# Layer 2's second products as seven products of halves, its narrow block first

## The chip, the cores and the metric

One NeuronCore of a Trainium2 chip runs the whole program. It has five engines that work beside each other and wait for each other by semaphores: TensorE (PE in the profile) multiplies and writes to PSUM, VectorE (DVE) and ScalarE (ACT) work element by element, SyncE (SP) issues the DMA transfers, and GpSimd (POOL) has nothing to do here. The metric is the device time of one execution in microseconds, the median of three runs.

## The reference

Attention with two kinds of masks (four heads see the last 32 positions, four see every 32nd), then two MLPs on the 2304 tokens that it gives, each with a squared relu:

```
attn = softmax(mask(q @ k.T / 8)) @ v            # 4 batches, 8 heads, 576 positions, 64 wide
x    = attn as (2304, 512)
x    = relu(x @ moe_w_in)**2  @ moe_w_out         # 512 -> 2048 -> 512
out  = relu(x @ moe2_w_in)**2 @ moe2_w_out        # 512 -> 2048 -> 512
```

## The kernel before

Numbers are split in two: a high part, rounded to the format fp32r in which TensorE multiplies here, and a low part, the remainder. A product of two numbers is three products on TensorE, high by high, low by high and high by low. So each value that TensorE reads is made in two operations: ScalarE copies it to fp32r (the high part), VectorE subtracts that from the value (the low part).

An MLP layer runs over blocks of 512 tokens and one narrow block of 256 (BLOCKS), and in a block over 16 pieces f of 128 of the 2048 hidden columns; a narrow block takes two pieces in one step. One step is

- the first product, mm1: 12 products of 512 columns (24 of 256 in a narrow block) into a PSUM bank ps_h. Then ScalarE takes the relu (r), ScalarE and VectorE each square it (gh, the high part, and sq), and VectorE makes the low part gl = sq - gh;
- the second product, mm2: 12 products of 512 columns that add up over the 16 steps in four PSUM banks ps_y. In layer 2 the squared values are the stationary operand and w_out streams; in layer 1 the other way round. At a block's end ScalarE copies the banks out (o) and a DMA stores them.

The main loop issues mm1(s + 1) before mm2(s), so that one step's products cover the making of the next step's values. Every engine takes its instructions in the order in which the code issues them (there is no scheduler), so that order is written by hand: attention of later batches, loading and conversion of weights and the splitting of layer 2's input (load_y, split_y, which read layer 1's result back from y_dram) are put in at numbered places (point) between groups of products.

Weights arrive as 64-bit words; a piece of 128 x 512 is converted in four operations in a row (sign_and_end: two on VectorE; exponent_range: ScalarE; together: VectorE; in_parts: a copy on ScalarE and a subtraction on VectorE), each piece one place behind the next. Layer 2's 32 pieces are loaded during layer 1's last block and converted there and in layer 2's first block. Attention takes the first three blocks along.

SBUF is nearly full, so buffers are shared under tags: x tiles (three pairs), the attention's buffers (qk0, qk1, qk2), the squared values (gh, gl, two each).

## Time and profile before

| | before |
|---|---|
| median of three runs | 909.28 us (909.27 to 909.30) |
| profiled execution | 909.87 us |
| its span, first to last instruction | 908.1 us |
| TensorE busy | 888.9 us, 98% |
| VectorE busy | 461.6 us, 51% |
| ScalarE busy | 410.3 us, 45% |
| mean granted TensorE clock | 0.994 of full |

The busy time of TensorE counts a product from its start to its modelled end, and products overlap; what one costs in a stream is read from the distance of two starts. Times on the clock of the trace are microseconds from the span's start. Layer 2 begins at about 508 us; its wide blocks run to about 856 us, its narrow block is the last.

### The profile page before, as it was taken

How to read it: one execution, taken by the hardware profiler on the slowest of the kernel's cores; microseconds unless marked ns; L12 is line 12 of the kernel's file. 1: busy time of each engine (PE TensorE's matmuls, PEld its weight loads, DVE VectorE, ACT ScalarE, POOL GpSimd, SP SyncE). 2: the span in 40 equal slices, each digit the busy share in tenths (PEclk: the TensorE clock that was granted, in tenths of full speed). 3: DMA queues.
4: the chain of work that ended last, by engine and by line, in shares of the span. 5: the costliest groups of instructions: out<-in, count | busy, mean ns of one | idle time of the engine just before them, and what ended most of it. 6: DMA issues, size and time to landing. Idle time of an engine off the chain costs nothing.

```text
span 908.1 us, 12461 instructions
## 1 busy us (share of the span) xinstructions
PE 888.9 (98%) x4640; PEld 750.1 (83%) x4640; DVE 461.6 (51%) x1201; ACT 410.3 (45%) x859; POOL 0.2 (0%) x4
## 2 busy tenths in 40 slices
PE   8699999999999999999999999999999999999998
PEld 8578878888888888899888888888888888888897
DVE  5999973477666665222378786322232222223221
ACT  6787863555555544322466766232233222322222
POOL 0000000000000000000000000000000000000000
PEclk9799999999999999999999999999999999999999
DMA  8956510222222120101666500010001000100010
GB/s 268 323 196 215 193 41 19 85 75 93 71 69 102 53 64 11 42 6 37 205 211 203 198 29 24 0 70 1 24 0 70 1 24 1 58 6 6 7 41 24
DMA packets 43885, 71.92 MB, mean 79 GB/s; under 512 B 3504, under 2 KB 28208, under 8 KB 43824
## 3 DMA queue, kind: packets, MB, share of 16 engines
q1 hardware_dynamic: 43824, 71.12, 23.5%
q8 instruction: 37, 0.61, 0.3%
q14 instruction: 24, 0.20, 0.1%
HBM read 61.67 MB, written 9.44 MB: 78 GB/s over the span
## 4 chain that ended last, share of the span: by engine, by line
PE 87%; DVE 9%; ACT 1%; DMA 1%; issue 1%; SPq 0%; ACTq 0%; DVEq 0%
PE ps_h L679 41%; PE ps_y L736 40%; PE ps_o L480 2%; DVE raw L219 2%; DVE w L244 1%; DVE val L230 1%; PE ps_pt L464 1%; PE ps_s L327 1%; DVE raw L216 1%; PE ps_s L421 1%; DVE s L441 1%; DMA qk<-st_qk_d 1%; DVE gl L703 1%; PE ps_x L526 1%; DVE xl L568 0%
## 5 line engine op out<-in xcount | busy, mean ns | idle before, releaser
L679 PE MATMUL ps_h<-xh,w 128*128 128x512 f32 (+1 forms) x1280 | 402.4, 374 | 0.0
L679 PEld LDWEIGHTS ps_h<-xh,w 128*128 128x128 f32 x1280 | 234.2, 189 | 38.5
L693 ACT ACTIVATE r<-ps_h 128x512 f32<-128x512 f32 x144 | 86.1, 598 | 373.1 <-PE ps_h L679 340.8
L702 DVE TENSOR_TENSOR sq<-r 128x512 f32<-128x512 f32 x110 | 76.1, 692 | 336.7 <-ACT r L693 336.6
L679 PE MATMUL ps_h<-xl,w 128*128 128x512 f32 (+1 forms) x640 | 236.5, 370 | 0.0
L736 PE MATMUL ps_y<-gh,w 128*128 128x512 f32 (+1 forms) x640 | 157.5, 376 | 0.0
L736 PE MATMUL ps_y<-w,gh 128*128 128x512 f32 x576 | 144.6, 389 | 0.0
L679 PEld LDWEIGHTS ps_h<-xl,w 128*128 128x128 f32 x640 | 121.3, 190 | 17.3
L736 PEld LDWEIGHTS ps_y<-w,gh 128*128 128x128 f32 x576 | 107.6, 188 | 22.0
L703 DVE TENSOR_TENSOR gl<-sq,gh 128x512 fp32r<-128x512 f32 x144 | 99.7, 692 | 49.8 <-ACT gh L699 36.0
L736 PEld LDWEIGHTS ps_y<-gh,w 128*128 128x128 f32 x640 | 108.2, 188 | 16.5
L736 PE MATMUL ps_y<-gl,w 128*128 128x512 f32 (+1 forms) x320 | 85.4, 374 | 0.0
L736 PE MATMUL ps_y<-w,gl 128*128 128x512 f32 x288 | 79.1, 389 | 0.0
L701 ACT ACTIVATE gh<-r 128x512 fp32r<-128x512 f32 x110 | 69.7, 634 | 3.5
L736 PEld LDWEIGHTS ps_y<-w,gl 128*128 128x128 f32 x288 | 54.1, 188 | 11.3
L736 PEld LDWEIGHTS ps_y<-gl,w 128*128 128x128 f32 x320 | 54.5, 188 | 8.5
L457 ACT ACTIVATE s<-s,m 96x128 f32<-96x128 f32 (+2 forms) x176 | 55.7, 387 | 4.4 <-DVE m L441 3.8
L225 ACT ACTIVATE raw<-raw 128x512 f32<-128x512 f32 x64 | 43.2, 675 | 13.3 <-DVE raw L219 13.3
L480 PEld LDWEIGHTS ps_o<-v,pt 128*96 128x96 f32 (+2 forms) x352 | 42.8, 174 | 7.1 <-ACT pt L472 2.4
L219 DVE SCALAR_TENSOR_TENSOR raw<-raw 128x512 int32<-128x512 int32 x64 | 44.4, 694 | 2.2
L244 DVE TENSOR_TENSOR w<-val,w 128x512 fp32r<-128x512 f32 x64 | 43.7, 683 | 2.6 <-ACT w L243 2.5
L230 DVE SCALAR_TENSOR_TENSOR val<-raw 128x512 int32<-128x512 int32 x64 | 43.7, 684 | 0.0
(39 smaller groups left out, 576.0 us busy)
## 6 DMA issues: line engine op xcount, KB each, us to landing
raw<-moe_w_in_d SPq DMA_DIRECT2D x32, 512.0 KB, 4.9
raw<-moe_w_out_d SPq DMA_DIRECT2D x32, 512.0 KB, 3.9
qk<-loc_qk_d SPq DMA_DIRECT2D x12, 416.0 KB, 3.1
out_d<-o SPq DMA_DIRECT2D x18, 256.0 KB, 2.0
y_dram<-o SPq DMA_DIRECT2D x16, 256.0 KB, 2.0
y_in<-y_dram SPq DMA_DIRECT2D x16, 256.0 KB, 3.0
qk<-loc_qk_d SPq DMA_DIRECT2D x12, 304.0 KB, 4.0
v<-loc_v_d SPq DMA_DIRECT2D x24, 130.0 KB, 2.4
```

The source lines that it names most:

```text
L219: nc.vector.scalar_tensor_tensor(out=lower, in0=upper, scalar=-(2 ** 31), in1=lower, op0=ALU.bitwise_and, op1=ALU.bitwise_or)
L225: nc.scalar.activation(out=upper, in_=upper, func=AF.Copy, scale=2.0 ** (W_EXP // 8 - 112))
L230: nc.vector.scalar_tensor_tensor(out=val[n].bitcast(I32), in0=upper, scalar=3, in1=lower, op0=ALU.logical_shift_left, op1=ALU.bitwise_or,)
L244: nc.vector.tensor_tensor(out=w[:, 1], in0=v, in1=r32(w[:, 0]), op=ALU.subtract)
L457: nc.scalar.activation(out=blk, in_=blk, func=AF.Exp, scale=-1.0, bias=m[:nq, j:j + 1])
L480: nc.tensor.matmul(ps[:nq, j * W:(j + 1) * W], lhsT=pt[:nk, j * nq:(j + 1) * nq], rhs=t[:nk, j * W:(j + 1) * W], start=True, stop=True,)
L679: nc.tensor.matmul(ps[:, e * n:(e + 1) * n], lhsT=w[:, a, c * P:(c + 1) * P], rhs=x[:, c, :n], start=c == 0 and e == 0 and i == 0, stop=c ...
L693: nc.scalar.activation(out=r, in_=ps, func=AF.Relu, scale=W_BACK)
L701: nc.scalar.activation(out=h, in_=r, func=AF.Square)
L702: nc.vector.tensor_tensor(out=sq, in0=r, in1=r, op=ALU.mult)
L703: nc.vector.tensor_tensor(out=lo, in0=sq, in1=r32(h), op=ALU.subtract)
L736: nc.tensor.matmul(y, lhsT=lhsT, rhs=rhs, start=f == 0 and c not in seen, stop=end and m == last[c])
```

## The change

Layer 2's narrow block comes first, and its second product stays as it was, by another way to its operands. In the four wide blocks of layer 2 two steps (an even and an odd f, 256 hidden columns, a pair) are taken together: the 512 x 256 squared values are cut in two by tokens (even and odd) and in two by hidden columns, w_out's 256 x 512 in two by two, and Strassen's scheme makes the product of seven products of halves instead of eight. Each of the seven has its own accumulator bank over the block: four ps_y banks and the three ps_a banks, so that one bank, ps_h, is left for the first products. For each pair VectorE and ScalarE make the sums and differences of the squared values and split them in high and low parts: g_first for the first three products, g_second for the other four. The sums of w_out's pieces are made once, when they are converted (halves), and kept as float32; their high and low parts are made anew for each pair (w_operands; w_direct in the narrow block) into the x tile that layer 2 leaves free. At a block's end seven operations on VectorE (sums) put the output together from the seven banks. The conversion of weights uses all eight places of a step in layer 1's last block instead of six.

```diff
-    [(0, TB), (TB, TB), (2 * TB, TB), (3 * TB, TB), (NT - TB // 2, TB // 2)],
+    [(0, TB // 2)] + [(n * TB + TB // 2, TB) for n in range(4)],
...
+QK_COLS = {"qk0": 1024, "qk1": 1024, "qk2": 768}
+HALF = DM // 2
...
+    def halves(n):
+        kind, layer, f = pieces[n]
+        w = wt[pieces[n]] = wpool.tile([P, 4, HALF], F32, tag=f"w{n % half1}", name="wf")
+        v = val.pop(n).rearrange("p (h m) -> p h m", h=2)
+        sub = nc.vector.tensor_tensor
+        if f % 2 == 0:
+            nc.scalar.activation(out=w[:, 0:4:3], in_=v, func=AF.Copy)
+            sub(out=w[:, 1], in0=v[:, 1], in1=v[:, 0], op=ALU.subtract)
+        else:
+            w0 = wt["out", 1, f - 1]
+            nc.scalar.activation(out=w[:, 0:2], in_=v, func=AF.Copy)
+            sub(out=w0[:, 2], in0=v[:, 1], in1=w0[:, 3], op=ALU.subtract)
+            sub(out=w[:, 2], in0=v[:, 1], in1=w0[:, 1], op=ALU.subtract)
+            sub(out=w[:, 3], in0=w[:, 2], in1=v[:, 0], op=ALU.subtract)
...
+    def x_tile(part, n):
+        return xpool.tile([P, KC, TB], F32R, tag=f"{part}{n}", name=part)
     def x_tiles(j):
         if j not in xh:
-            xh[j] = x_tile("xh", "xh")
-            xl[j] = x_tile("xl", "xl")
+            xh[j], xl[j] = (x_tile(t, j % 3) for t in ("xh", "xl"))
...
-        if s != 1 and n_att[0] < len(att):
+        if s == first_7 + 1 or s != 1 and s < first_7 and n_att[0] == len(att):
+            ps = ps_a.tile([P, TB], F32, tag="a", name="ps_h")
...
+        if s >= first_7:
+            t = sqs[s] = gpool.tile([P, TB], F32, tag=("r", "sq")[s % 2], name="sq", bufs=1)
+            nc.scalar.activation(out=t, in_=ps, func=AF.Relu, scale=W_BACK)
+            nc.vector.tensor_tensor(out=t, in0=t, in1=t, op=ALU.mult)
+            return
...
+    sqs, ga, gb, w_parts, rings, banks = {}, {}, {}, {}, {}, {}
+    first_7 = steps.index((NB + 1, 0))
+    PA, PB = ("11", "s1t1", "s3t3"), ("12", "s4b22", "s2t2", "a22t4")
+    def ring(n):
+        if n not in rings:
+            rings[n] = [x_tile(t, n).rearrange("p c n -> p (c n)") for t in ("xh", "xl")]
+        return rings[n]
+    def w_direct(s):
+        f = steps[s][1]
+        w_parts[s] = []
+        for e in range(2):
+            at = (s % 2 * 2 + e) * 512
+            hi, lo = (x[:, at:at + 512] for x in ring(2))
+            w = ready(("out", 1, f + e))
+            src = w[:, 0:2] if e else w[:, 0:4:3]
+            h3, l3 = (x.rearrange("p (h m) -> p h m", h=2) for x in (hi, lo))
+            parts(h3, l3, src)
+            w_parts[s].append((hi, lo))
...
+    def w_operands(s, first):
+        k, f = steps[s]
+        n = 1 if k == len(blocks) - 1 and f % 4 == 1 else 2
+        wr = w_parts[s] = [x[:, 48:48 + 7 * HALF] for x in ring(n)]
+        w = ready(("out", 1, f - 1)), ready(("out", 1, f))
+        src, a, e = (w[0][:, 0:3], 0, 3) if first else (w[1], 3, 7)
+        hi, lo = (x[:, a * HALF:e * HALF] for x in wr)
+        parts(hi, lo, src.rearrange("p i m -> p (i m)"))
+    def quarters(s):
+        return [t.rearrange("p (n e) -> p e n", e=2) for t in (sqs[s - 1], sqs[s])]
+    def parts(hi, lo, src):
+        nc.scalar.activation(out=hi, in_=src, func=AF.Copy)
+        nc.vector.tensor_tensor(out=lo, in0=src, in1=r32(hi), op=ALU.subtract)
+    def g_first(s):
+        a1, a2 = quarters(s)
+        n = TB // 2
+        h = fpool.tile([P, 3 * HALF], F32R, tag="qk2", name="gah", bufs=1)
+        lo = gpool.tile([P, 3 * HALF], F32R, tag="gl", name="gal", bufs=2)
+        h, lo = ga[s] = [x.rearrange("p (i n) -> p i n", i=3) for x in (h, lo)]
+        s13, s42 = (
+            gpool.tile([P, TB + P], F32, tag="gh", name="s", bufs=2)[:, :2 * n].rearrange(
+                "p (i n) -> p i n", i=2)
+            for _ in range(2)
+        )
+        parts(h[:, 0], lo[:, 0], a1[:, 0])
+        tt = nc.vector.tensor_tensor
+        tt(out=s13[:, 0], in0=a1[:, 1], in1=a2[:, 1], op=ALU.add)
+        tt(out=s13[:, 1], in0=a1[:, 0], in1=a1[:, 1], op=ALU.subtract)
+        nc.scalar.activation(out=h[:, 1:3], in_=s13, func=AF.Copy)
+        tt(out=s42[:, 1], in0=s13[:, 0], in1=a1[:, 0], op=ALU.subtract)
+        tt(out=lo[:, 1:3], in0=s13, in1=r32(h[:, 1:3]), op=ALU.subtract)
+        tt(out=s42[:, 0], in0=a2[:, 0], in1=s42[:, 1], op=ALU.subtract)
+        gb[s] = s42
+    def g_second(s):
+        _, a2 = quarters(s)
+        s42 = gb[s]
+        h = fpool.tile([P, 4 * HALF], F32R, tag="qk0", name="gbh", bufs=1)
+        lo = fpool.tile([P, 4 * HALF], F32R, tag="qk1", name="gbl", bufs=1)
+        h, lo = gb[s] = [x.rearrange("p (i n) -> p i n", i=4) for x in (h, lo)]
+        parts(h[:, 0:4:3], lo[:, 0:4:3], a2)
+        parts(h[:, 1:3], lo[:, 1:3], s42)
+        if steps[s][0] < len(blocks) - 1 or steps[s][1] == 1:
+            w_operands(s, False)
...
+    def products(s, which, point):
+        k, f = steps[s]
+        nt = TB // 2 // P
+        first, end = f == 1, f == NF - 1
+        wr = w_parts[s]
...
+        if first:
+            tags = ("y0", "y1", "y2") if which == 0 else ("y3", "a", "a", "a")
+            for name, tag in zip(names, tags):
+                pool = ps_a if tag == "a" else ps_y
+                banks[name] = pool.tile([P, 512], F32, tag=tag, name="ps_y")
+        at = range(len(names)) if which == 0 else (2, 0, 3, 1)
+        for i in at:
+            y = banks[names[i]]
+            cols = slice((w0 + i) * HALF, (w0 + i + 1) * HALF)
+            for t in range(nt):
+                rows = slice(t * P, (t + 1) * P)
+                for m, (a, w) in enumerate(((h, wr[0]), (h, wr[1]), (lo, wr[0]))):
+                    nc.tensor.matmul(
+                        y[:, t * HALF:(t + 1) * HALF],
+                        lhsT=a[:, i, rows],
+                        rhs=w[:, cols],
+                        start=first and t == 0 and m == 0,
+                        stop=end and t == nt - 1 and m == 2,
+                    )
+            point()
+            if end:
+                sums(k, names[i])
...
+        if name == "11":
+            acc["p1"] = tile_of("pt")
+            nc.scalar.activation(out=acc["p1"], in_=banks[name], func=AF.Copy, scale=W_BACK)
+        elif name == "s2t2":
+            u2, u3, c22 = acc["u2"], acc["u3"], acc["c22"] = tile_of("pt"), tile_of("s"), tile_of("s")
+            add(u2, name, acc["p1"])
+            add(u3, "s3t3", u2)
+            add(c22, "s1t1", u3)
+            store(c22, 1, 1)
+            add(u2, "s1t1", u2)
+        elif name == "12":
+            add(acc["p1"], name, acc["p1"])
+            store(acc["p1"], 0, 0)
+        elif name == "a22t4":
+            add(acc["u3"], name, acc["u3"], -1.0)
+            store(acc["u3"], 1, 0)
+        elif name == "s4b22":
+            add(acc["u2"], name, acc["u2"])
+            store(acc["u2"], 0, 1)
...
+    def layer_2(s, point):
+        k, f = steps[s]
+        if s < first_7:
+            if s + 1 < first_7:
+                w_direct(s + 1)
+            mm2(s, point)
+        elif f % 2 == 0:
+            g_first(s + 1)
+            if s == first_7:
+                w_operands(s + 1, True)
+            else:
+                products(s - 1, 1, point)
+            g_second(s + 1)
+        else:
+            products(s, 0, point)
+            if s + 1 == len(steps):
+                products(s, 1, point)
+                return
+            w_operands(s + 2, True)
+            if steps[s + 2][0] == len(blocks) - 1 and steps[s + 2][1] > 1:
+                w_operands(s + 2, False)
...
-        s -= 12
+        s, lag, each = (first[NB], 2, 1) if k == NB + 1 else (s - 12, 3, 2)
...
-                elif (layer == 1 or j == NB - 1 and f > 2) and n_pt[0] % 4:
+                elif j == NB - 1 and f > 2 and layer == 0 or layer == 1 and n_pt[0] % 4:
...
-            mm1(s + 1, point)
+            if s == first[NB] - 1:
+                w_direct(s + 1)
+            if s != first_7:
+                mm1(s + 1, point)
+            if s == first_7 - 1:
+                mm1(s + 2, point)
             point()
-            mm2(s, point)
+            if layer == 0:
+                mm2(s, point)
+            else:
+                layer_2(s, point)
```

How the instructions stand, at three places.

VectorE in a steady part of a wide block of layer 2, before: two steps, with sq the square and gl its low part, and between them the low part of a piece of the next block's input.

```order
L702 TENSOR_TENSOR sq<-r 128x512
L703 TENSOR_TENSOR gl<-sq,gh 128x512
L654 TENSOR_TENSOR xl_6861<-y_in,xh_6860 128x512
L702 TENSOR_TENSOR sq<-r 128x512
L703 TENSOR_TENSOR gl<-sq,gh 128x512
```

The same place in the change, one pair of steps: gal and gbl are the low parts of the squared values' operands for the first three and the last four products, s their sums and differences, xl <- wf the low parts of the weights' operands.

```order
L824 TENSOR_TENSOR gbl<-sq,gbh 128x2x256
L824 TENSOR_TENSOR gbl<-s,gbh 128x512
L824 TENSOR_TENSOR xl<-wf,xh 128x1024
L717 TENSOR_TENSOR sq<-sq 128x512
L824 TENSOR_TENSOR xl<-wf,xh 128x768
L717 TENSOR_TENSOR sq<-sq 128x512
L824 TENSOR_TENSOR gal<-sq,gah 128x256
L839 TENSOR_TENSOR s<-sq 128x256
L840 TENSOR_TENSOR s<-sq 128x256
L842 TENSOR_TENSOR s<-s,sq 128x256
L843 TENSOR_TENSOR gal<-s,gah 128x512
L844 TENSOR_TENSOR s<-sq,s 128x256
```

The four operations of two steps became twelve of a pair, and the low part for the first three products stands behind sums that need the pair's second square.

ScalarE at a boundary of two blocks of layer 2, before: r is the relu, gh is the squared value's high part, o the four copies of the finished block to the output.

```order
L693 ACTIVATE r<-ps_h 128x512
L701 ACTIVATE gh<-r 128x512
L745 ACTIVATE o<-ps_y 128x512 x4
L693 ACTIVATE r<-ps_h 128x512
L701 ACTIVATE gh<-r 128x512
```

ScalarE where the change goes from the narrow block to the first wide one: xh <- wf are the high parts of weights, sq <- ps_h the relu of the first two steps, gah and gbh the high parts of the operands.

```order
L823 ACTIVATE xh<-wf 128x512 x2
L723 ACTIVATE r<-ps_h 128x512
L731 ACTIVATE gh<-r 128x512
L823 ACTIVATE xh<-wf 128x512 x2
L716 ACTIVATE sq<-ps_h 128x512 x2
L773 ACTIVATE o<-ps_y 128x512 x2
L823 ACTIVATE gah<-sq 128x256
L841 ACTIVATE gah<-s 128x512
L823 ACTIVATE xh<-wf 128x768
L823 ACTIVATE gbh<-sq 128x2x256
L823 ACTIVATE gbh<-s 128x512
L823 ACTIVATE xh<-wf 128x1024
```

The narrow block's two output copies now stand between the second relu and the first operand of the first three products, and the weights' high part behind those.

VectorE at a boundary of two wide blocks in the change (before, nothing but sq and gl of the steps stands there, as in the first fence of this section): the seven operations L897 are the sums that read the old block's accumulators.

```order
L717 TENSOR_TENSOR sq<-sq 128x512
L824 TENSOR_TENSOR gal<-sq,gah 128x256
L839 TENSOR_TENSOR s<-sq 128x256
L840 TENSOR_TENSOR s<-sq 128x256
L842 TENSOR_TENSOR s<-s,sq 128x256
L843 TENSOR_TENSOR gal<-s,gah 128x512
L844 TENSOR_TENSOR s<-sq,s 128x256
L897 SCALAR_TENSOR_TENSOR o<-ps_y,o 128x512 x7
L824 TENSOR_TENSOR gbl<-sq,gbh 128x2x256
L824 TENSOR_TENSOR gbl<-s,gbh 128x512
L824 TENSOR_TENSOR xl<-wf,xh 128x1024
```

The sums stand behind the new block's first operands and ahead of its other ones.

## Rows read from the trace of the kernel before

**Rows 1.** The page: busy time of each engine, and the granted clock in 40 slices.

```profile
PE 888.9 (98%) x4640; PEld 750.1 (83%) x4640; DVE 461.6 (51%) x1201; ACT 410.3 (45%) x859; POOL 0.2 (0%) x4
...
PEclk9799999999999999999999999999999999999999
```

**Rows 2.** The page: the chain that ended last, share of the span by line.

```profile
PE ps_h L679 41%; PE ps_y L736 40%; PE ps_o L480 2%; DVE raw L219 2%; DVE w L244 1%; DVE val L230 1%; PE ps_pt L464 1%; PE ps_s L327 1%; DVE raw L216 1%; PE ps_s L421 1%; DVE s L441 1%; DMA qk<-st_qk_d 1%; DVE gl L703 1%; PE ps_x L526 1%; DVE xl L568 0%
```

**Rows 3.** Stretches: us, then busy time of each engine, clock, DMA share, GB/s.

```profile
433.00:510.00 77.00, 77.00 (x341) 63.79 (x340) 52.35 (x91) 48.02 (x82) 0.00 (x0) 1.00 0.61 206
565.00:852.00 287.00, 287.00 (x1268) 237.68 (x1267) 80.80 (x120) 78.24 (x132) 0.00 (x0) 1.00 0.06 21
```

**Rows 4.** Timeline of TensorE, a wide step of layer 2: start, duration, instruction.

```profile
590.06 0.39 PE L679 MATMUL ps_h<-xh,w 128*128 128x512 f32 x1
...
595.50 0.39 PE L679 MATMUL ps_h<-xh,w 128*128 128x512 f32 x1
```

**Rows 5.** Timeline of TensorE, a step of layer 2's narrow block.

```profile
856.62 0.28 PE L679 MATMUL ps_h<-xh,w 128*128 128x256 f32 x1
...
859.49 0.63 PE L736 MATMUL ps_y<-w,gh 128*128 128x512 f32 x2
...
862.24 0.28 PE L679 MATMUL ps_h<-xh,w 128*128 128x256 f32 x1
```

**Rows 6.** Timeline of TensorE, second product of layer 1's narrow block.

```profile
384.95 2.00 PE L736 MATMUL ps_y<-gh,w 128*128 128x256 f32 x16
...
387.69 0.28 PE L679 MATMUL ps_h<-xh,w 128*128 128x256 f32 x1
```

**Rows 7.** Groups by line and shape, 508 to 908 us: busy us, mean ns.

```profile
L736 PEld LDWEIGHTS ps_y<-w,gh 128*128 128x128 f32 x576 | 107.6, 188 | 22.0
...
L701 ACT ACTIVATE gh<-r 128x512 fp32r<-128x512 f32 x63 | 39.9, 634 | 2.0
...
L230 DVE SCALAR_TENSOR_TENSOR val<-raw 128x512 int32<-128x512 int32 x15 | 10.3, 685 | 0.0
...
L654 DVE TENSOR_TENSOR xl<-y_in,xh 128x256 fp32r<-128x256 f32 x4 | 1.7, 418 | 0.0
L653 ACT ACTIVATE xh<-y_in 128x256 fp32r<-128x256 f32 x4 | 1.6, 401 | 0.0
```

**Rows 8.** Timeline of VectorE, the stretch where weights are converted.

```profile
475.25 0.69 DVE L703 TENSOR_TENSOR gl<-sq,gh 128x512 fp32r<-128x512 f32 x1 [1.88 <-ACT gh L699]
...
476.47 0.42 DVE L216 TENSOR_SCALAR raw<-raw 128x512 int32<-128x512 int32 x1
476.92 0.70 DVE L219 SCALAR_TENSOR_TENSOR raw<-raw 128x512 int32<-128x512 int32 x1
477.54 0.69 DVE L654 TENSOR_TENSOR xl<-y_in,xh 128x512 fp32r<-128x512 f32 x1
478.14 0.69 DVE L230 SCALAR_TENSOR_TENSOR val<-raw 128x512 int32<-128x512 int32 x1
```

**Rows 9.** Timeline of all engines around the end of a first product.

```profile
853.89 1.98 PE L736 MATMUL ps_y<-w,gh 128*128 128x512 f32 x8
854.14 0.60 ACT L693 ACTIVATE r<-ps_h 128x512 f32<-128x512 f32 x1 [4.18 <-PE ps_h L679]
...
854.78 0.69 DVE L702 TENSOR_TENSOR sq<-r 128x512 f32<-128x512 f32 x1 [3.92 <-ACT r L693]
...
855.60 0.69 DVE L703 TENSOR_TENSOR gl<-sq,gh 128x512 fp32r<-128x512 f32 x1
```

**Rows 10.** Timeline, the last instruction of an engine.

```profile
904.49 0.60 ACT L745 ACTIVATE o<-ps_y 128x512 f32<-128x512 f32 x1 [0.76 <-PE ps_y L736]
```

**Rows 11.** Three stretches of 2.5 us near the start.

```profile
17.50:20.00 2.50, 1.16 (x14) 1.00 (x13) 1.45 (x10) 2.20 (x8) 0.00 (x0) 1.00 0.96 315
35.00:37.50 2.50, 1.19 (x8) 0.84 (x7) 2.40 (x8) 2.11 (x6) 0.00 (x0) 0.50 0.63 221
42.50:45.00 2.50, 2.50 (x7) 1.94 (x6) 2.47 (x6) 1.42 (x5) 0.00 (x0) 0.50 1.02 349
```

More of the change, by code (lines that the diff above doesn't have):

```diff
@@ L48 @@
 START_ATT = 1
-GAP = 80
+GAP = 52
 N_WARM = 8
@@ L159, in tile_attention_then_two_mlps @@
     vpool = ctx.enter_context(tc.tile_pool(name="values", bufs=2))
[L160 removed]
+    xpool = ctx.enter_context(tc.tile_pool(name="x", bufs=1))
     fpool = ctx.enter_context(tc.tile_pool(name="fills", bufs=5))
+    vfpool = ctx.enter_context(tc.tile_pool(name="fillv", bufs=5))
     apool = ctx.enter_context(tc.tile_pool(name="att", bufs=2))
@@ L238, in together @@
         del raw[n]
+    def halves(n):
[12 more added lines that the diff above has]
+            sub(out=w[:, 3], in0=w[:, 2], in1=v[:, 0], op=ALU.subtract)
     def in_parts(n):
+        if pieces[n][:2] == ("out", 1):
+            halves(n)
+            return
         w = wt[pieces[n]] = wpool.tile([P, 2, 512], F32R, tag=f"w{n % half1}", name="w")
@@ L295, in load_qk @@
         tag = "qk" + str(i % 3 if i < SPLIT else 0)
-        kin[i] = fpool.tile([P, QKW if tag == "qk2" else 4 * KW], F32, tag=tag, name="qk", bufs=1)
+        kin[i] = fpool.tile([P, QK_COLS[tag]], F32, tag=tag, name="qk", bufs=1)
         nc.sync.dma_start(out=kin[i][:, :qk.shape[-1]], in_=qk)
@@ L303, in split_qk @@
         w, kw = ng * nq, (ng - 1) * ks + P
-        qs = fpool.tile([P, QKW], F32R, tag="qk2", name="qs", bufs=1)
-        k2 = fpool.tile([P, 2, 2 * KW], F32R, tag="qk1", name="k2", bufs=1)
+        qs = fpool.tile([P, QK_COLS["qk2"]], F32R, tag="qk2", name="qs", bufs=1)
+        k2 = fpool.tile([P, 2, 512], F32R, tag="qk1", name="k2", bufs=1)
         qk_parts[i] = qs, k2
@@ L643, in load_y @@
         if c == 0:
-            xin[k] = [x_tile(t, t + "2") for t in ("xh", "xl")]
+            xin[k] = [x_tile(t, (k - NB) % 2) for t in ("xh", "xl")]
         t = y_in[k, c] = apool.tile([P, TB], F32, tag="s", name="y_in")
@@ L694, in mm1 @@
         h = gpool.tile([P, TB + P], F32R, tag="gh", name="gh", bufs=2)[:, g0:g0 + TB]
-        lo = gpool.tile([P, TB + P], F32R, tag="gl", name="gl", bufs=2)[:, g0:g0 + TB]
+        lo = gpool.tile([P, 3 * HALF], F32R, tag="gl", name="gl", bufs=2)[:, g0:g0 + TB]
         if 0 < n_load[0] - n_part[0]:
@@ L710, in mm2 @@
         ne = tiles_of(k)
-        ws = [ready(("out", layer, f + e)) for e in range(ne)]
+        ws = w_parts.pop(s) if layer else [ready(("out", layer, f + e)) for e in range(ne)]
         h, lo = gh.pop(s), gl.pop(s)
-        ny = KC if layer == 0 else n // P
+        ny = n // P if layer else KC
         if f == 0:
@@ L723, in mm2 @@
                     g0 = e * n
-                    rows = slice(g0 + c * P, g0 + (c + 1) * P)
                     if layer == 1:
-                        todo.append((i, c, y, gp[:, rows], w[:, a]))
+                        todo.append((i, c, y, gp[:, g0 + c * P:g0 + (c + 1) * P], w[a]))
                     else:
@@ L741, in mm2 @@
             if end and m == last[c]:
-                t = apool.tile([P, 512], F32, tag="pt", name="o")
-                if layer == 0:
-                    t = t[:, :n]
-                nc.scalar.activation(out=t, in_=y, func=AF.Copy, scale=W_BACK)
-                if layer == 0:
-                    nc.sync.dma_start(out=y_dram[:, c, t0:t0 + n], in_=t)
-                else:
-                    nc.sync.dma_start(out=out[t0 + c * P:t0 + (c + 1) * P, :], in_=t)
+                no = 512 if layer else n
@@ L750, in mm2 @@
+                t = apool.tile([P, 512], F32, tag="pt", name="o")[:, :no]
+                nc.scalar.activation(out=t, in_=y[:, :no], func=AF.Copy, scale=W_BACK)
+                to = out[t0 + c * P:t0 + (c + 1) * P, :] if layer else y_dram[:, c, t0:t0 + n]
+                nc.sync.dma_start(out=to, in_=t)
             if m in places:
                 point()
+    sqs, ga, gb, w_parts, rings, banks = {}, {}, {}, {}, {}, {}
+    first_7 = steps.index((NB + 1, 0))
+    PA, PB = ("11", "s1t1", "s3t3"), ("12", "s4b22", "s2t2", "a22t4")
@@ new lines, in g_second @@
+    def g_second(s):
[13 more added lines that the diff above has]
+        wr = w_parts[s]
+        (h, lo), names, w0 = (ga.pop(s), PA, 0) if which == 0 else (gb.pop(s), PB, 3)
+        if first:
[20 more added lines that the diff above has]
+                sums(k, names[i])
@@ new lines, in tile_attention_then_two_mlps, with sums, tile_of, add @@
+    acc = {}
+    def sums(k, name):
+        def tile_of(tag):
+            return apool.tile([P, 512], F32, tag=tag, name="o")
+        def add(dst, src, to, sign=1.0):
+            nc.vector.scalar_tensor_tensor(
+                out=dst, in0=banks[src], scalar=sign * W_BACK, in1=to, op0=ALU.mult, op1=ALU.add
+            )
+        def store(t, half, c):
+            t0, n = BLOCKS[1][blocks[k][1]]
+            dst = out[t0:t0 + n, c * HALF:(c + 1) * HALF].rearrange("(a p e) m -> e p a m", p=P, e=2)
+            nc.sync.dma_start(out=dst[half], in_=t.rearrange("p (a m) -> p a m", a=2))
+        if name == "11":
[17 more added lines that the diff above has]
+            store(acc["u2"], 0, 1)
@@ L756, in tile_attention_then_two_mlps @@
     for k, s in first.items():
-        s -= 12
+        s, lag, each = (first[NB], 2, 1) if k == NB + 1 else (s - 12, 3, 2)
         for i, fn in enumerate((load_y, split_y)):
             for c in range(KC):
-                y_at.setdefault(s + 3 * i + 2 * c, []).append((fn, k, c))
+                y_at.setdefault(s + lag * i + each * c, []).append((fn, k, c))
     spans = [((b * NF or START_ATT) * N_PT, ((b + 1) * NF - 1) * N_PT - 4) for b in range(3)]
```

7 lines of the change are left out of this document (3 added, 4 removed).

## The prediction

> **What bounds the kernel now.** I read the page's busy shares and slices first: TensorE is busy 98% of the span, at a granted clock of 9 tenths or more in nearly every slice [rows 1]. The chain that ended last runs 41% of the span through the first products and 40% through the second [rows 2]. So time is won only by shortening TensorE's own stream, and lost wherever it is made to wait. The stretch table says what the other two engines have to spare there: in layer 2's four wide blocks (565 to 852 us) TensorE is busy 287 of 287 us, VectorE 81 and ScalarE 78; in the stretch before (433 to 510 us), where layer 2's weights are converted, VectorE is already busy 52 of 77 [rows 3]. Then I read TensorE's order of time in one wide step: 24 products of 512 columns between 590.06 and 595.50, 5.44 us or 0.2267 each [rows 4].
>
> **What the change removes: 20.6 us of TensorE.** Two wide steps (a pair) have 24 second products of 512 columns now: 24 x 0.2267 = 5.44 us. Strassen's seven halves take 7 x 2 x 3 = 42 products of 256 columns. The price of one is not half of 0.2267, and the trace has two prices for it: layer 2's narrow block runs 24 of them in its first product from 856.62 to 859.49, 0.1197 each [rows 5]; layer 1's narrow block runs 24 in its second product from 384.95 to 387.69, 0.1142 each [rows 6]. I take the second. The difference between them that I find in the program is where the streamed operand starts: in layer 1's narrow second product it starts 48 floats into its tile (g0 = 48), in the first products at a multiple of 128 floats, as the stationary operand does; the new operands are cut with the same 48. That this is the reason is a reading, so 0.1197 stays the upper end. 42 x 0.1142 = 4.80, so a pair saves 0.64 us, and 32 pairs (four blocks of eight) 20.6 us; by 0.1197 it would be 13.2.
>
> A rule of the Trainium skill speaks against this. Every product keeps its own weight load, and those loads take 188 ns [rows 7], yet the products of rows 6 follow each other in 114, so two loads and products overlap. The Trainium skill (TensorE: Matmul & The Clock Gate, "The mechanism") says that a weight load overlaps with products in flight only if it targets another row group; here each takes the whole array, so by it the 18 added loads of a pair would stand in the open. The trace disagrees, with 114 against 188 ns.
>
> **What a pair asks of VectorE and ScalarE.** Prices of a 512-wide operation: 0.69 on VectorE, 0.60 to 0.63 on ScalarE; of a 256-wide one 0.42 and 0.40 [rows 7, 9]. From these an estimate for 768: 0.96 and 0.87; for 1024: 1.23 and 1.10. On VectorE operations that don't wait for each other start 0.60 apart, not 0.69 (477.54 and 478.14) [rows 8]; so 256-wide ones 0.34 apart. Strided sources cost little: the word operation at L230 reads every second word and takes 0.68 [rows 7]. VectorE has twelve operations in a pair, ScalarE eight: summed 7.7 and 5.5 us in a pair of 10.24 us (two first products 2 x 2.72, and 4.80). Neither becomes the bound by its sum; what decides is whether each result is there in time. I lay out a pair from the start of the odd first product:
>
> TensorE: odd first product 0 to 2.72, the last four products of the pair before to 5.46, the next even first product to 8.18, the first three products to 10.24. From the start of the product that follows a first product to ScalarE's relu there are 0.25 us (853.89 to 854.14), and VectorE follows within 0.04 [rows 9]. So ScalarE's relu is at 2.97 to 3.57, VectorE's square to 4.30, its remainder of the first quarter to 4.63, the two sums to 5.30, ScalarE's copy of them to 5.97, VectorE's remainder 6.02 to 6.71. TensorE wants it at 8.18: 1.5 us of room. The last four products' operands: copies on ScalarE to 6.62 and 7.70, the weights' 1024 columns to 8.80; VectorE's remainders to 8.44 and 10.08; wanted at 10.24 + 2.72 = 12.96. The first product has one PSUM buffer now instead of three: the next odd one, at 10.24, waits for the relu of the even one, which ScalarE reaches after the 1024 columns, 8.80 to 9.40; in the four pairs of a block that also split y_in, about 9.9. Room 0.8 or 0.3 us. The weights' first 768 columns wait for the first three products to end (10.24) and are done on VectorE at about 12.3, wanted at 18.4. So a steady pair has no wait, and its extra 10 or so operations cost nothing as long as TensorE's 10.24 us cover them.
>
> **What it adds: 8.4 us.**
> *First pair, 2.2 us.* Its first products come after only the last narrow step's second product and one first product (2 x 2.72 = 5.44 us from the end of the odd first product), and ScalarE's queue has the narrow block's two output copies ahead of the first quarter. The second ends 2.72 + 0.25 + 0.60 = 3.57; quarter 3.97; VectorE's remainder and two sums to 5.09; copy 5.14 to 5.76; remainder 5.8 to 6.5 and one difference; only then the weights' 768 columns (ScalarE until about 6.6), 6.75 to 7.7. The second product wants them: TensorE stands from 5.55 to 7.75.
> *Three block boundaries, 3.3 us.* The seven sums that read the old accumulators stand in VectorE's queue behind the new block's first half (free at 6.96 of the layout). They start at 6.96, 7.78, 8.60 and 9.20 (dependent ones start 0.82 apart, as the square and remainder of rows 9, 854.78 and 855.60). The second accumulator is read by the third and fourth, until 9.9; TensorE wants to start it anew at 8.18 + 0.69 = 8.87. It waits 1.1 us, three times. The remaining sums end at 11.7 and push the 1024-wide remainder to 14.05, which is wanted at 14.15: no second wait, with nothing to spare.
> *The end, 2.9 us.* After the last first product the two halves follow the layout with less cover: they wait 0.38 for the remainder of the sums (4.04 against 3.66) and 0.35 for the remainder of the differences. The products then end 8.3 us after the last first product; VectorE's seven sums, which begin when the first of the four is done (6.5), end at 11.3, 3.0 after TensorE. Now ScalarE's last copy starts at 904.49, so the last product ended about 904.24; the copy ends at 905.09, 0.8 after it, and the span 3.0 later [rows 10]; the new stores are of the same 256 KB. So 2.2 more there, and 0.7 of waits.
> *At no price:* the narrow block costs 5.62 us a step wherever it stands [rows 5]. Its weight copies (two of 512 on each engine a step) and the conversion lie beside products. The conversion is the tight one: from layer 1's last block on, eight of its operations a step instead of six. Two steps then ask VectorE for two remainders, four each of the three word operations, two remainders of w_in, four 256-wide differences, half a split: 10.9 us by starts 0.60 and 0.45 apart [rows 8], against 10.88 of TensorE. The remainder gl may start 4.2 us late (it is ready 4.95 us into a step and wanted only by the last third of the next step's second product, at 9.97 with its own 0.7), so I take nothing. If that cover is gone (VectorE 5% to 10% slower through waits for ScalarE), 13 such steps run 3.5 to 7 us late, and TensorE loses up to 3, with the narrow block's steps that follow up to 5.
>
> **The sum.** -20.6 + 2.2 + 3.3 + 2.9 = -12.2 us: the span goes from 908.1 to 895.9. The profiled execution took 909.87 us, 0.6 above the median of 909.28; the same 12.2 from the median give **897.1 us**.
>
> **Rivals.**
> (a) *Products of 256 columns cost 0.1197.* For it: that is the price in the same layer, with the same pattern of operands, high, low, high. Against it: the 48 floats. 1344 x 0.0055 = 7.4 more: 904.5 us.
> (b) *VectorE is late in the conversion stretch.* For it: 10.9 of 10.88 us. Against it: 4.2 us of room, and before it a step's gl even waits for ScalarE by up to 1.88 us [rows 8]. 898.5 to 902.
> (c) *The clock falls in the first pair's wait.* In 35.0 to 37.5 us, with TensorE busy 1.19 of 2.50 us, it was granted at 0.50 (1.2 GHz), and still at 0.50 in 42.5 to 45.0, although TensorE was busy throughout; but with 1.16 of 2.50 busy at 17.5 to 20.0 it stayed at 1.00 (2.4 GHz) [rows 11]. 2.5 us at half speed cost 1.3, twice that 2.5: 898.5 to 900.
> (d) *Slower than before: every pair waits for its own first half.* The place is the remainder of the two sums, seven dependent operations after the first product, on two engines. For it: nothing of this chain is in the trace, and each link's handover is read from one pair of operations. Against it: 1.5 us of room. It decides when the chain is 1.9 us longer than laid out (1.5 of room and 12.2 / 32 = 0.38 of gain), 0.27 per link; with 2.1 more it is 0.6 a pair, 916 us.
> (e) *The loads stand in the open.* With 188 ns as the least distance of two products a pair has 42 x 0.188 = 7.9 us instead of 5.44: 2.46 x 32 = 79 more, with the 8.4 above 997 us. Rows 6 speak against it. This is what the Trainium skill's rule on row groups (above) would come to.
>
> **Chances.** Forecast (892 to 900) 0.52; (a) 0.16; (b) 0.14; (c) 0.06; (d) 0.07, and 0.04 for a weaker form of it that ends within 0.2% of 909.28 (1.8 us, about what a measurement of this kernel can tell from no change); (e) 0.01. The range 892 to 904.5 takes in the forecast, (a), (b) and (c), 0.88: its low end is no wait at the boundaries and a half of it in the first pair, its high end the price 0.1197. Faster 0.88, same 0.04, slower 0.08.
>
> **What the profile would show.** Right: products of 256 columns with gah, gal, gbh, gbl about 0.114 apart and a pair in 10.24 us; one TensorE wait near 2 us where layer 2's first wide block begins, released by VectorE; waits near 1 us at three block boundaries; VectorE near 75% and ScalarE above 50% in the wide blocks; no TensorE wait for gl before. Wrong: a pair of 10.5 us without waits is (a); waits in every pair for gal or for ps_h are (d); a clock below 1.00 after the first wait is (c); waits for gl or w between about 440 and 550 us are (b).

## The result, and the profile after

The changed kernel takes 901.73 us (median of 4 runs, 901.01 to 902.72) against 909.29 before (4 runs on the same chip, 909.27 to 909.87): a ratio of 0.9908, 95% interval 0.9896 to 0.9920. So it is faster, by 0.9%, and inside the range; but 7.6 us were gained where 12.2 were forecast. The profiled execution took 901.71 us with a span of 899.8, which is 8.3 below the span before. The question is where some 4 us of the forecast went.

The page of the changed kernel, its head and TensorE's clock, answers to [rows 1]:

```profile
span 899.8 us, 14022 instructions
PE 875.2 (97%) x5216; PEld 764.8 (85%) x5216; DVE 631.2 (70%) x1521; ACT 491.8 (55%) x987; POOL 0.2 (0%) x4
PEclk9799999999999999999999999999999999999999
```

TensorE is still the bound, at a granted clock of 9 tenths or more from the third slice on. What it does in one pair of steps is read from its timeline (start, duration, instruction), with the first row of each group:

```profile
602.13 0.28 PE L877 MATMUL ps_y<-xh,gbh 128*128 128x256 f32 x1
...
604.96 0.39 PE L704 MATMUL ps_h<-xh,w 128*128 128x512 f32 x1
...
607.68 0.28 PE L877 MATMUL ps_y<-xh,gah 128*128 128x256 f32 x1
...
609.80 0.39 PE L704 MATMUL ps_h<-xh,w 128*128 128x512 f32 x1
...
612.52 0.28 PE L877 MATMUL ps_y<-xh,gbh 128*128 128x256 f32 x1
```

The last four products of a pair take 2.83 us (602.13 to 604.96, 24 products), the first three 2.12 (607.68 to 609.80, 18): 0.1178 each, neither of the two prices that the prediction weighed. A pair is 10.39 us (602.13 to 612.52), not 10.24, and there is no wait in it. The places with waits, in the same timeline, are layer 2's first pair and the block boundaries (the first of three is shown):

```profile
561.30 0.39 PE L704 MATMUL ps_h<-xh,w 128*128 128x512 f32 x1
...
564.99 0.38 PE L877 MATMUL ps_y<-xh,gah 128*128 128x256 f32 x1 [0.81 <-ACT xh L823]
566.19 0.39 PE L877 MATMUL ps_y<-xl,gah 128*128 128x256 f32 x1 [0.82 <-DVE xl L824]
...
568.24 0.39 PE L704 MATMUL ps_h<-xh,w 128*128 128x512 f32 x1
...
649.23 0.28 PE L877 MATMUL ps_y<-xh,gah 128*128 128x256 f32 x1
...
650.73 0.36 PE L877 MATMUL ps_y<-xh,gah 128*128 128x256 f32 x1 [0.63 <-DVE o L897]
...
652.19 0.39 PE L704 MATMUL ps_h<-xh,w 128*128 128x512 f32 x1
```

In the first pair twelve first products take 3.69 instead of the 2.72 of 604.96 to 607.68, and the 18 behind them 3.25 instead of 2.12: 0.97 + 1.13 = 2.10 us. At the boundary 18 products take 2.96 instead of 2.12, 0.84; the other two boundaries lose 0.87 each. At the end the timeline of all engines has:

```profile
885.23 0.28 PE L877 MATMUL ps_y<-xh,gbh 128*128 128x256 f32 x1
...
891.76 4.53 DVE L897 SCALAR_TENSOR_TENSOR o<-ps_y,o 128x512 f32<-128x512 f32 x7 [0.89 <-PE ps_y L877]
...
893.43 0.28 PE L877 MATMUL ps_y<-xh,gbl 128*128 128x256 f32 x1
```

and the kernel before, its last row of products:

```profile
903.84 0.62 PE L736 MATMUL ps_y<-w,gl 128*128 128x512 f32 x2
```

The last 66 products take 8.20 us from the first start to the last instead of 65 x 0.1178 = 7.66, so 0.54 is waited; VectorE's seven sums end at 896.29, 2.58 after the last product (893.71), and the span ends 3.5 after that.

The account closes. From the start of layer 2 (508.46 before, 508.18 now):

| term | forecast, us | measured, us |
|---|---|---|
| 32 pairs' second products | -20.6 | 32 x (4.95 - 5.44) = -15.7 |
| first pair's wait | +2.2 | +2.1 |
| three boundaries | +3.3 | +2.6 |
| end: waits, sums, store | +2.9 | 0.54 + 2.45 = +3.0 |
| start of layer 2 | 0 | -0.3 |
| sum | -12.2 | -8.3 |

(2.45 is the distance from the last product's end to the span's end, 6.09, less the same before, 3.64, where the last product ended at 904.46 by its row. In the seven changed kernels of this document layer 2 begins between 507.61 and 508.54, so the -0.3 at its start can't be told from chance.) One term is off by 4.9 us, the price of a product; the others together are off by 1 us in the other direction.

### The profile page after: what moved, and what is told of

Same layout as the page of the kernel before. It is cut to its first block, busy times and chain, and to the rows that moved or that the text cites. A ratio compares the mean times of both kernels' runs of the same rounds, so it can differ in the third digit from the quotient of the medians.

```text
span 899.8 us, 14022 instructions
## 1 busy us (share of the span) xinstructions
PE 875.2 (97%) x5216; PEld 764.8 (85%) x5216; DVE 631.2 (70%) x1521; ACT 491.8 (55%) x987; POOL 0.2 (0%) x4
## 4 chain that ended last, share of the span: by engine, by line
PE 83%; DVE 12%; ACT 2%; issue 1%; DMA 0%; SPq 0%; DVEq 0%; ACTq 0%
PE ps_h L704 40%; PE ps_y L765 21%; PE ps_y L877 16%; PE ps_o L503 2%; DVE raw L223 2%; DVE w L268 2%; DVE val L234 2%; PE ps_pt L487 1%; PE ps_s L351 1%; DVE s L464 1%; DVE raw L220 1%; DVE o L897 1%; PE ps_s L444 1%; DVE gl L733 1%; PE ps_x L549 1%
## 5 line engine op out<-in xcount | busy, mean ns | idle before, releaser
L824 DVE TENSOR_TENSOR xl<-wf,xh 128x768 fp32r<-128x768 f32 (+1 forms) x80 | 79.9, 1009 | 18.3 <-ACT xh L823 18.0
L823 ACT ACTIVATE xh<-wf 128x768 fp32r<-128x768 f32 (+1 forms) x80 | 68.9, 880 | 27.4 <-PE ps_y L877 27.4
L717 DVE TENSOR_TENSOR sq<-sq 128x512 f32<-128x512 f32 x64 | 44.0, 688 | 53.7 <-ACT sq L716 53.7
L877 PE MATMUL ps_y<-xh,gbl 128*128 128x256 f32 x256 | 72.0, 281 | 0.1
L877 PE MATMUL ps_y<-xl,gbh 128*128 128x256 f32 x256 | 71.9, 281 | 0.0
L877 PE MATMUL ps_y<-xh,gbh 128*128 128x256 f32 x256 | 71.9, 281 | 0.0
L733 DVE TENSOR_TENSOR gl<-sq,gh 128x512 fp32r<-128x512 f32 x80 | 55.2, 690 | 21.2 <-ACT gh L729 15.2
L877 PE MATMUL ps_y<-xh,gah 128*128 128x256 f32 x192 | 54.2, 283 | 2.7 <-DVE o L897 1.9
L877 PE MATMUL ps_y<-xl,gah 128*128 128x256 f32 x192 | 54.0, 281 | 0.8 <-DVE xl L824 0.8
L877 PE MATMUL ps_y<-xh,gal 128*128 128x256 f32 x192 | 54.0, 281 | 0.0
```

The costliest lines, as they stand in the source:

```text
L717: nc.vector.tensor_tensor(out=t, in0=t, in1=t, op=ALU.mult)
L733: nc.vector.tensor_tensor(out=lo, in0=sq, in1=r32(h), op=ALU.subtract)
L823: nc.scalar.activation(out=hi, in_=src, func=AF.Copy)
L824: nc.vector.tensor_tensor(out=lo, in0=src, in1=r32(hi), op=ALU.subtract)
L877: nc.tensor.matmul(y[:, t * HALF:(t + 1) * HALF], lhsT=a[:, i, rows], rhs=w[:, cols], start=first and t == 0 and m == 0, stop=end and t == ...
```

## The experiments

Three theories for the price of 0.1178 were set against each other: the order of the products (A), the start of the streamed operand (B), and what the products ahead leave behind (C). Times below are medians; each is compared with the kernel before on its own chip, so the ratio is what to compare with 0.9908. The executions of one kernel spread by 0.6 to 3.4 us, so what a change of 1 or 2 us consists of is read from the traces.

**The remainder's products last.** In the 24 pairs that neither start nor end a block:

```diff
+        todo = []
...
+                    todo.append((i, t, m, a[:, i, rows], w[:, cols]))
+        if not (first or end):
+            todo.sort(key=lambda x: x[2] == 2)
...
```

> In the changed kernel a product of 256 columns costs 0.1178 us, neither the 0.1142 of layer 1's narrow block nor the 0.1197 of the first products. In layer 1's narrow block the products with the remainder as operand come last in a step (sorted), in its last step and in the changed kernel they come third of every three. Here the 24 pairs that neither start nor end a block have the remainder's products last as well. Theory A (this order sets the price): 24 x 42 = 1008 products fall from 0.1178 to 0.114, 3.8 us, to about 898. Theory B (where the streamed operand starts sets it) and theory C (the stream takes over a state from the 512-column products ahead of it): still 0.1178, 901.7.

902.94 us against 909.92, ratio 0.9912 (0.9896 to 0.9928). Groups of 18 and 24 still take 2.12 and 2.83 us. The order does nothing to the price: theory A falls.

**Start at 0 floats.**

```diff
-        wr = w_parts[s] = [x[:, 48:48 + 7 * HALF] for x in ring(n)]
+        wr = w_parts[s] = [x[:, 0:7 * HALF] for x in ring(n)]
```

> The weights' operands start at 0 floats of their tile instead of 48. Theory B (the start of the streamed operand sets the price): all 1344 products go from 0.1178 to the 0.1197 to 0.1200 of the first products, 2.6 to 3.0 us more, about 904.5. Theory A (the order alone): 0.1178 still, 901.7.

906.04 us against 909.92, ratio 0.9952 (0.9934 to 0.9969), the span 3.7 us longer than the changed kernel's. TensorE's timeline of a pair:

```profile
602.56 0.28 PE L877 MATMUL ps_y<-xh,gbh 128*128 128x256 f32 x1
...
605.43 0.40 PE L704 MATMUL ps_h<-xh,w 128*128 128x512 f32 x1
...
608.18 0.28 PE L877 MATMUL ps_y<-xh,gah 128*128 128x256 f32 x1
...
610.33 0.40 PE L704 MATMUL ps_h<-xh,w 128*128 128x512 f32 x1
```

The groups take 2.87 and 2.15 us instead of 2.83 and 2.12 (behind the first two products 0.1200 from start to start), so the start matters (theory B). It is a little more than was expected, because the twelve first products behind each group take 2.75 instead of 2.72 as well: a pair is 10.52 us instead of 10.39. But B alone doesn't explain why 48 floats give 0.1178 here and 0.1142 in [rows 6].

**Products alone.** One kernel with nothing but groups of 48 products of 256 columns, each behind 12 of 512 (named "between"), with the start of the streamed operand in the group's name; "last" has the remainder's products last.

> Products alone; attention and both layers are left out, the output holds a product of the first input. Groups of 48 products of 256 columns, each behind 12 of 512, for starts of the streamed operand of 0, 16, 32, 48, 64, 80 and 96 floats, the remainder's products third of every three or last; groups of 24 of 512 columns at the same starts; and two groups behind a wait for VectorE. Theory A: 0.1178 for third of three, 0.114 for last, at every start or at all but 0. Theory B: 0.1197 at 0, the same price for both orders at 48. Theory C: a group behind a wait runs at another price than the same group without. For 512 columns 0.2267 at every start, by all three.

TensorE's timeline (the distance of two rows' starts, over the count, is the price):

```profile
84.17 5.92 PE L68 MATMUL mixed_at0f<-big 128*128 128x256 f32 x48
89.92 2.91 PE L46 MATMUL between<-big 128*128 128x512 f32 x12
...
135.03 5.82 PE L68 MATMUL mixed_at48f<-big 128*128 128x256 f32 x48
140.69 2.88 PE L46 MATMUL between<-big 128*128 128x512 f32 x12
143.41 5.82 PE L68 MATMUL last_at48f<-big 128*128 128x256 f32 x48
149.06 2.88 PE L46 MATMUL between<-big 128*128 128x512 f32 x12
...
203.42 5.80 PE L68 MATMUL waited_at0f<-big 128*128 128x256 f32 x47
209.05 2.91 PE L46 MATMUL between<-big 128*128 128x512 f32 x12
212.35 0.38 PE L68 MATMUL waited_at48f<-big,z 128*128 128x256 f32 x1 [0.39 <-DVE z L82]
212.57 5.50 PE L68 MATMUL waited_at48f<-big 128*128 128x256 f32 x47
217.91 2.90 PE L46 MATMUL between<-big 128*128 128x512 f32 x12
```

From 0 floats 5.75 us for 48, 0.1198; from 32 5.76; from 48 in both orders 5.66 and 5.65, 0.1178 (from 16 as well, and 64, 80, 96 repeat 0, 16, 32). Behind a wait for VectorE 47 products from 48 floats take 5.34 us, 0.1136, while from 0 the wait changes nothing (5.63, 0.1198). So the start sets which prices are possible, and what came ahead picks one of them: B and C together. For 512 columns all three theories had expected 0.2267 at every start, which did not hold (last section). The changed kernel's own trace has the lower price too: behind the last wait in its tail, the same kind of products as above follow each other faster:

```profile
891.73 0.28 PE L877 MATMUL ps_y<-xh,gbl 128*128 128x256 f32 x1
```

From there to the last product (893.43, above) are fifteen products in 1.70 us, 0.1133 each.

**What ahead of a group brings the lower price.**

> Products alone again (attention and both layers left out). Each group stands behind 12 products of 512 columns with both operands at multiples of 128 floats. The first such run gave 0.1178 for 256 columns streamed from 48 floats, and 0.1133 for the same behind a wait; from 0 floats 0.1200 with and without a wait; the order of the products did nothing. Here a few products of another kind stand ahead of the group instead of a wait (1 to 4 of 256 columns from 0, 16, 32 or 48 floats, 1 of 128 or 64 columns, 1 of 512 from 48 or 16). Theory C1 (the distance that the products ahead leave between a weight load and the stream is kept): some of these bring 0.1133, those of 256 columns from 0 above all, since layer 1's narrow block runs at 0.1142 behind such. Theory C2 (only an idle TensorE changes it): all stay at 0.1178. Behind a wait, 512 columns from 48 floats: 0.2200 if they too lose 16 cycles, 0.2267 if not. Starts of 8, 24, 40 and 56 floats and a held operand from 48 floats are looked at, 0.113 to 0.120 by either.

The same kind of timeline; "ahead" stands between the 12 products and the group:

```profile
42.66 5.82 PE L44 MATMUL none_x<-big 128*128 128x256 f32 x48
48.31 2.88 PE L44 MATMUL between<-big 128*128 128x512 f32 x12
51.03 0.40 PE L44 MATMUL ahead<-big 128*128 128x256 f32 x2
51.27 5.62 PE L44 MATMUL ahead2of256at0x<-big 128*128 128x256 f32 x48
56.73 2.90 PE L44 MATMUL between<-big 128*128 128x512 f32 x12
```

Two products of 256 columns from 0 floats ahead: 5.46 us instead of 5.65 for 48; after the first four they are 0.1133 apart. Three or four of them, one from 16 or 32 floats, one of 64 columns, and one of 512 from 48 floats do the same; one of 256 from 0, two from 48, one of 128 columns, and one of 512 from 16 don't. TensorE need not stand idle for it: C2 falls. What C1 forecast came, but not for every such product, and what it gives as the reason, a distance between load and stream that is kept, no run shows. Of the other starts (8, 16, 24, 32, 40, 56), with or without a wait, none came below 0.1167 (8 floats, without). For 512 columns, 48 floats behind a wait cost 5.37 / 23 = 0.2335 (163.08 to 168.45), neither of the two values expected: dearer than the 0.2267 of [rows 4], so there is nothing to win there.

**The lower price in the kernel.** The last of twelve first products is cut into two of 256 columns:

```diff
+                    final = c == KC - 1 and i == 2 and e == ne - 1
+                    cuts = (0, HALF, n) if final and s >= first_7 else (0, n)
+                    for at, to in zip(cuts, cuts[1:]):
...
```

> The last of the twelve first products of 512 columns is cut into two of 256, so that the second products stand behind two products of 256 columns from 0 floats, as the groups did in the second run of products alone, which then ran at 0.1133 instead of 0.1178. By that run a group gains 4.45 ns a product (80 ns for 18, 107 for 24), and pays 5 for the cut, about 16 for its first four products and 15 for the first four of 512 columns behind it: 44 and 71 ns, 31 times each, 3.6 us less than the changed kernel: 898.1. Rival (what the products alone showed does not hold beside VectorE's and ScalarE's traffic): products stay at 0.1178 and the cut costs 0.3 us, 902.0.

900.01 us against 909.74, ratio 0.9892 (0.9879 to 0.9906), between the theory and the rival. TensorE's timeline of a pair:

```profile
603.06 0.29 PE L879 MATMUL ps_y<-xh,gbh 128*128 128x256 f32 x1
...
605.79 0.39 PE L706 MATMUL ps_h<-xh,w 128*128 128x512 f32 x1
...
608.54 0.29 PE L879 MATMUL ps_y<-xh,gah 128*128 128x256 f32 x1
...
610.60 0.39 PE L706 MATMUL ps_h<-xh,w 128*128 128x512 f32 x1
```

The groups fall from 2.83 and 2.12 to 2.74 and 2.06 us, a pair from 10.39 to 10.28 with its cut and what it costs behind: nearly all of the 3.6 us is there in the pairs, 31 x 0.11 = 3.4. The span fell by 1.7 only. Part of the rest is in its first pair, in the stretch table (us, busy time of PE, PEld, DVE, ACT, POOL, then the granted clock):

```profile
562.50:565.00 2.50, 1.67 (x8) 1.11 (x6) 2.14 (x6) 1.82 (x3) 0.00 (x0) 1.00 0.91 297
565.00:567.50 2.50, 1.71 (x10) 1.71 (x11) 2.50 (x4) 2.05 (x4) 0.00 (x0) 0.76 0.05 17
567.50:570.00 2.50, 2.50 (x12) 2.36 (x12) 1.18 (x2) 0.59 (x1) 0.00 (x0) 0.55 0.00 0
```

In this execution the clock fell behind the first pair's two waits, to 0.55, close to 0.50 (1.2 GHz), and the 18 products there took 4.58 us instead of the changed kernel's 3.25, the twelve first products behind them 3.05 instead of 2.74: 1.6 us. The three boundaries lose 0.97 each, 0.1 more than in the changed kernel. The changed kernel's profiled execution has the same two waits and a clock of 1.00 in all these stretches. That the whole 3.6 us would have come without the fall isn't shown: the fastest execution, with a mean clock of 0.993, took 899.44 us, 1.6 less than the changed kernel's fastest (901.01).

**The waits, moved.** The weights' 768 columns of the first pair ahead of the narrow block's output copies, and another order at a block's start:

```diff
-        at = range(len(names)) if which == 0 else (2, 0, 3, 1)
+        at = ((0, 2, 1) if first else (0, 1, 2)) if which == 0 else (2, 0, 3, 1)
...
+            else:
+                w_operands(s + 2, True)
...
-            if s == first_7:
-                w_operands(s + 1, True)
-            else:
+            if s > first_7:
                 products(s - 1, 1, point)
```

> The weights' 768 columns of layer 2's first pair are copied ahead of the narrow block's output copies, and at a block's start the second products run in the order 11, s3t3, s1t1, so that the accumulator that is read last is started last. By the waits read in the changed kernel (0.97 and 1.13 us in the first pair, 0.84, 0.87 and 0.87 at the three boundaries) and the room that each edit gives: the first pair's two waits fall to at most 0.3, the boundaries' to at most 0.25 each: 1.8 + 1.9 = 3.7 us less, 898.0. Rival: what is late is ScalarE's and VectorE's queue as a whole, and the same time is waited for the next operand: 901 to 902.

900.83 us against 909.92, ratio 0.9892 (0.9878 to 0.9907), the span 0.9 us shorter where 3.7 were expected: the rival, mostly. TensorE's timeline of the first pair, and that of all engines at the first boundary:

```profile
567.79 0.50 PE L704 MATMUL ps_h<-xh,w 128*128 128x512 f32 x1 [0.99 <-ACT sq L716]
...
653.21 1.22 DVE L824 TENSOR_TENSOR xl<-wf,xh 128x1024 fp32r<-128x1024 f32 x1
...
654.48 0.39 PE L877 MATMUL ps_y<-xl,gbh 128*128 128x256 f32 x1 [0.31 <-DVE xl L824]
```

Most of both waits came back at the next operand in the queue: the first product of the next step waits for the relu, which ScalarE reached only after the 1024 columns (0.99), and the products behind a boundary for the 1024 columns' remainder, which VectorE reached after the seven sums. 24 products there took 0.5 to 0.6 longer.

**Three sums later, the relu earlier.** On top of the last kernel:

```diff
-            if end:
+            if end and (i == 2 or which == 0 or s + 1 == len(steps)):
+                sums(k, names[i])
...
+            if f == 0 and s > first_7:
+                for name in ("12", "a22t4", "s4b22"):
+                    sums(k - 1, name)
...
-        if steps[s][0] < len(blocks) - 1 or steps[s][1] == 1:
+        if s > first_7 + 1 and (steps[s][0] < len(blocks) - 1 or steps[s][1] == 1):
...
+            if s == first_7 + 1:
+                w_operands(s, False)
```

> The run with the waits moved showed them come back one operand later: the second first product waited 0.99 for ScalarE's relu, which stood behind the weights' 1024 columns, and the last four products waited 0.5 to 0.6 for the remainder of the 1024 columns, which stood behind the seven sums. Here the 1024 columns of the first pair come after that relu too, and three of the seven sums come after the remainders. Theory (VectorE's and ScalarE's order, not their load, makes these waits): the first pair's waits fall from 2.1 to at most 0.4, each boundary's from 0.86 to at most 0.2, 3.5 to 4.3 us less than the changed kernel, 897.4 to 898.2. Rival (their load): again about 1 us is gained, 900.8.

897.88 us against 910.42, ratio 0.9866 (0.9850 to 0.9883). At the same boundary, all engines:

```profile
646.23 2.73 DVE L897 SCALAR_TENSOR_TENSOR o<-ps_y,o 128x512 f32<-128x512 f32 x4
...
650.08 1.22 DVE L824 TENSOR_TENSOR xl<-wf,xh 128x1024 fp32r<-128x1024 f32 x1
651.22 1.88 DVE L897 SCALAR_TENSOR_TENSOR o<-ps_y,o 128x512 f32<-128x512 f32 x3
```

The four sums that free accumulators stay ahead, three go behind the operands. A boundary now costs 0.10 us, the first pair 0.34 + 0.15. So it was the order of two queues, not their load.

**Both.**

> The cut of the last first product together with the later sums and the earlier weights of the run that gave 897.88: 3.6 us less than that if the gains add up, 894.3; as much as that run, 897.9, if the faster products only uncover a wait for VectorE (a pair falls from 10.39 to 10.27 us, with 7.7 us of work for VectorE).

895.63 us (5 runs, 894.76 to 896.42) against 909.74, ratio 0.9845 (0.9832 to 0.9859): the fastest of all, 1.5% below the kernel before. A pair is 10.28 us; its span is 2.2 below that of the run with the later sums, not 3.6: layer 2's products of halves begin 0.35 later, and the three boundaries (18 products in 2.29 us, 0.23 over the steady 2.06), with a step behind each, together lose some 0.6 more than there.

## Why the prediction was right, and where it was off

- **The products, -20.6 forecast, -15.7 measured.** The step that failed is the price: "I take the second". Its reading, that 48 floats make the difference between 0.1197 and 0.1142, is half of it: the run from 0 floats shows that the start matters. The other half is what stands ahead. Layer 1's narrow block reaches 0.1142 because its second products follow first products of 256 columns; layer 2's follow 512 columns. The trace of the kernel before already held that case, in the last step of layer 1's narrow block, whose second product follows the next block's first product of 512. TensorE's timeline of the kernel before:

```profile
418.56 2.00 PE L736 MATMUL ps_y<-gh,w 128*128 128x256 f32 x16
...
421.29 0.39 PE L679 MATMUL ps_h<-xh,w 128*128 128x512 f32 x1
...
424.03 0.64 PE L736 MATMUL ps_y<-gh,w 128*128 128x256 f32 x4
...
426.86 0.39 PE L679 MATMUL ps_h<-xh,w 128*128 128x512 f32 x1
```

  24 products take 2.73 us from 418.56, and 2.83 from 424.03: 0.1179, the price that the new products have. (The last step also has the remainder's products third of every three; the first experiment and the products alone show that this order does nothing.) With that price the sum would have been -12.2 + 4.8 = -7.4. Rival (a) had the direction and, with 0.1197, 1.5 times the size. That the time lay inside the range is owed to this rival, whose price was the upper end, and not to the price that was taken.
- **The first pair, 2.2 forecast, 2.1 measured.** Right in place and size. The forecast had one wait, at the second product for VectorE's remainder; there are two, since the first product streams ScalarE's 768 columns and waits for these already. The second starts 7.61 us behind the odd first product's end (558.58 to 566.19), 7.75 forecast.
- **The boundaries, 3.3 forecast, 2.6 measured.** Right in mechanism; the sums begin 6.89 us into the layout (6.96 forecast). All engines at the first boundary, where the odd first product started at 640.96:

```profile
647.85 4.53 DVE L897 SCALAR_TENSOR_TENSOR o<-ps_y,o 128x512 f32<-128x512 f32 x7
```

  In the trace the two sums that read the result just ahead of them start 0.72 and 0.73 behind it, not 0.82 as in [rows 9], the other four 0.60 to 0.61 behind the sum ahead; so the fourth, which frees the accumulator, ends at 9.6 and not at 9.9. That the second wait has "nothing to spare" is what the moved waits showed.
- **The end, 2.9 forecast, 3.0 measured.** The size is partly luck, since errors cancel: VectorE's sums end 2.58 after the last product (3.0 forecast), but the span ends 3.5 after the sums (3.0 forecast), and the last product of the kernel before ended at 904.46, not at about 904.24; waits come to 0.54 for the forecast 0.7.
- **No wait in a steady pair; rival (d) falls.** The sums' remainder is ready 6.64 us into the layout (646.91 to 647.60, with the odd first product from 640.96) against 6.71 laid out.
- **The conversion; rival (b) falls.** From 433 to 508 us TensorE is busy 75.00 of 75.00 us with VectorE at 62.40.
- **Rival (c)** didn't happen in the profiled execution; with the cut first product it did, in the one execution that has a trace, for 1.6 us in 18 products and the twelve behind them.
- **Rival (e) falls**: loads of 188 ns behind products 113 to 120 ns apart. The Trainium skill's rule on row groups (TensorE: Matmul & The Clock Gate, "The mechanism"), by which a load overlaps with products in flight only when its row group differs, would have each load wait; the trace disagrees, with these numbers. The same section also lets a load into a background weight buffer be pulled ahead; no run here shows whether that is what happens.

## What to carry to other kernels

Take the price of an instruction from a row where its neighbours, too, are those that it will have; if two rows differ by 5%, look for a third that has the new neighbourhood before naming a cause. Where an engine's queue has work that frees a buffer beside work that only ends a result, split it: what frees something goes first, the rest behind the next operands. A wait that is moved must be followed to the next operand in the same queue before its price is booked as won.

## What the runs showed of the chip that was not expected

- With a granted clock of 1.00 (2.4 GHz) a product of 256 columns with its own load of 128 cost 0.1133, 0.1178 or 0.1200 us from the starts of 0, 16 and 48 floats, by where the streamed operand starts (the starts of 0, 16 and 32 floats give the same prices as 64, 80 and 96, with the held operand at a multiple of 128) and by a wait or the few products ahead; the other starts tried averaged 0.1167 to 0.1202. Behind its first few products a group of these starts keeps its price to the end (48 measured). Worked out at 2.4 GHz, the three are 272, 283 and 288 cycles. With the held operand from 48 floats and the streamed one from 0 it is the same as the other way round: 48 products from 268.25 to 273.90 in the second run of products alone, 0.1177. With both from 48, behind a wait, 47 products take 5.62 us (286.24 to 291.86), 0.1196, close to the 0.1198 of both from 0: so it is not the streamed operand's start alone that counts, but how the two starts lie to each other. Why these prices arise wasn't settled.
- The Trainium skill (TensorE: Matmul & The Clock Gate, "Step-by-step: what each phase is for") describes two independent read ports for the streamed operand and the weights. That alone would not let the starts of the two matter to each other; in these runs they do, by up to 6%.
- For products of 512 columns every start tried (16, 32, 48, 80 and 96 floats) was dearer than 0 and 64, up to 0.2335 against 0.2267.
